# Seven block products of half width in place of four full ones: the second matrix product of an attention and feed-forward kernel

## The chip, the cores and the metric

The kernel runs on one core of one Trainium2 chip. The time is the core's execution time in microseconds (us), the median of several runs. The profile's span runs from the first to the last instruction and is about 2 us shorter than the time. Five engines matter here: TensorE (PE in the profile; its weight loads are PEld), VectorE (DVE), ScalarE (ACT), GpSimd (POOL) and SyncE, whose queue (SPq) issues most transfers.

## The reference, cut to what matters

```python
# batch 8, heads 8, sequence 576, head size 64; window 32
attn = softmax(mask(q @ k.T / 8)) @ v               # per head, only |i - j| <= 32
x    = attn.transpose(0, 2, 1, 3).reshape(4608, 512)
h    = x @ w_in                                      # 512 -> 2048
out  = gelu_tanh(h) @ w_out                          # 2048 -> 512, float32 out
```

## The kernel before

It works through nine tiles of 512 tokens. In tile t the first product (`ffn_in`: 16 x 4 matmuls of 512 columns) and gelu fill `gT`, 2048 features by 512 tokens in f16. The second product (`ffn_out`) makes 64 matmuls of 512 columns from it. Spread among those stands the attention of the next batch: scores (s), masks (m), weighing with the values (v: `ps_o` and `ps_d`), inversion on ScalarE, and spreading of the result into `xT` on VectorE (x). Queries and keys of the batch after that are cast on VectorE, transposed by transfers that SyncE issues, and wanted by the first score in the next second product.

```python
PLAN = {3: ([-1], [0]), 14: ([], [1]), 24: ([0], [2]), 35: ([1], [3]), 46: ([2], [4]), 58: ([3], [])}
# position in the 64 matmuls: (groups to weigh, invert and spread), (groups to score and mask)

def ffn_out(t, t4, fc):
    ...                                              # the last quarter of the last tile in two halves
        nc.tensor.matmul(py[:, cols], gTs[t][:, f, t4 * 128:t4 * 128 + 128],
                         w_out16[:, f, cols], start=(f == 0), stop=(f == NF - 1))
    if f == NF - 1:
        yo = yp.tile([128, 512], FP32, name="yo", tag="yo")
        (nc.scalar.copy if last and half == 0 else nc.vector.tensor_copy)(
            yo[:, cols], py[:, cols])
        ...                                          # one store for each contiguous run of output rows
            eng = nc.scalar if last and m else nc.sync if t else nc.gpsimd
            eng.dma_start(out_v[b, j, q0 + p:q0 + p + e, cols], yo[m:m + e, cols])
```

The softmax here doesn't subtract the row's maximum and nothing guards it: scores larger than these inputs give would overflow.

## Time and profile before

| | |
|---|---|
| time, median of 3 | 323.94 us (323.27 to 325.27) |
| profiled run | 325.46 us, span 323.7 us |
| TensorE busy | 311.7 us, 96% |
| VectorE busy | 136.0 us, 42% |
| one tile of 1 to 6 | 33.6 us: first product 13.8, second product with attention 19.8 |
| from TensorE's end to the end of the span | 3.6 us |

TensorE is busy nearly throughout, so the other engines matter only where TensorE waits for them, and at the end. The profiled run was 1.5 us slower than the median. Where those 1.5 us lie can't be told, as the other runs left no trace. (In the traces of all runs at full clock the start and tile 0 together vary between 60.35 and 63.30 us; tiles 2 to 6 of one kernel mostly repeat within 0.1 us.)

### The profile page before, as it was taken

What the parts mean: (1) busy time and instruction counts of PE and PEld (TensorE: products, weight loads), DVE (VectorE), ACT (ScalarE), POOL (GpSimd) and SP (SyncE); (2) the same over time, 40 slices, a digit from 0 to 9 for tenths busy, and PEclk for the clock granted to TensorE, in tenths of its full rate; (3) what the DMA queues carried; (4) which work ended last, traced back from release to release, by engine and by line L of the source; (5) the groups of instructions that cost most, each with busy time, mean ns of one, the idle gap of its engine ahead of it and who ended that gap; (6) DMA issues with size and microseconds to landing.
All of it is one profiled execution on the core that took longest, in us unless ns stands there. A gap on an engine that the chain in (4) does not pass through costs nothing.

```text
span 323.7 us, 5827 instructions
## 1 busy us (share of the span) xinstructions
PE 311.7 (96%) x2265; PEld 153.4 (47%) x2265; DVE 136.0 (42%) x290; ACT 201.8 (62%) x316; POOL 59.5 (18%) x82
## 2 busy tenths in 40 slices
PE   7688999999999999999999999999999999999995
PEld 2463545444554445444544454445444544444444
DVE  5655587641556064705570467034713530110011
ACT  1757577578667766777577766777668577705600
POOL 3646356292031101300040104010000000000000
PEclk9959999999999999999999999999999999999999
DMA  7999998999989596949495979799270220031022
GB/s 208 259 362 362 381 277 230 251 161 157 248 155 160 95 245 159 169 88 251 115 155 116 221 161 135 134 203 183 75 122 17 67 58 9 0 91 41 0 60 70
DMA packets 120490, 50.57 MB, mean 156 GB/s; under 512 B 100784, under 2 KB 112048, under 8 KB 120464
## 3 DMA queue, kind: packets, MB, share of 16 engines
q1 hardware_dynamic: 88752, 45.07, 58.2%
q0 software_dynamic: 31520, 4.98, 21.0%
q8 instruction: 17, 0.28, 0.4%
q10 hardware_dynamic: 192, 0.16, 0.2%
q14 instruction: 9, 0.07, 0.1%
HBM read 37.62 MB, written 9.44 MB: 145 GB/s over the span
## 4 chain that ended last, share of the span: by engine, by line
PE 93%; SPq 2%; DMA 2%; DVE 1%; ACT 0%; issue 0%; POOL 0%; POOLq 0%
PE mm L461 39%; PE mm L439 24%; PE ph L439 14%; PE ps_o L381 5%; PE ps_s L348 5%; PE ps_d L381 4%; DMA vr<-in_v_dram 2%; SPq L126 1%; PE py L461 1%; ACT gT L443 0%; SPq L135 0%; PE pt L277 0%; DVE w_out L186 0%; PE pt L279 0%; DVE KT L285 0%
## 5 line engine op out<-in xcount | busy, mean ns | idle before, releaser
L461 PE MATMUL mm<-w_out,gT 128*128 128x512 f16 (+1 forms) x576 | 132.0, 377 | 0.8 <-DVE w_out L186 0.8
L439 PE MATMUL mm<-xT,w_in 128*128 128x512 f16 x360 | 89.0, 382 | 0.0
L439 PEld LDWEIGHTS <-w_in 128*128 128x128 f16 x576 | 56.2, 98 | 68.6 <-DVE w_in L186 1.5
L461 PEld LDWEIGHTS <-gT 128*128 128x128 f16 x592 | 54.2, 98 | 61.8 <-issue 0.6
L443 ACT ACTIVATE gT<-mm 128x512 f16<-128x512 f32 x90 | 53.7, 597 | 35.5 <-PE mm L439 35.5
L439 PE MATMUL ph<-xT,w_in 128*128 128x512 f16 x216 | 57.3, 381 | 1.2 <-ACT gT L443 1.2
L354 ACT ACTIVATE pe<-ps_s 128x704 f16<-128x704 f32 x64 | 43.3, 727 | 9.9 <-PE ps_s L348 9.2
L395 ACT ACTIVATE lt<-ps_d 128x480 f32<-128x480 f32 (+3 forms) x40 | 22.2, 555 | 43.2 <-PE ps_d L381 43.1
L443 ACT ACTIVATE gT<-ph 128x512 f16<-128x512 f32 x54 | 32.2, 597 | 13.3 <-PE ph L439 13.3
L405 DVE TENSOR_TENSOR xT<-ps_o,lt 128x480 f16<-128x480 f32 (+5 forms) x38 | 20.3, 552 | 46.9 <-ACT lt L396 46.8
L411 DVE TENSOR_TENSOR xT<-ps_o,lt 128x384 f16<-128x384 f32 (+1 forms) x8 | 4.3, 541 | 80.7 <-ACT lt L396 80.7
L363 DVE TENSOR_TENSOR pe<-pe,mask 128x704 f16<-128x704 f16 x64 | 34.4, 543 | 6.3 <-ACT pe L354 4.0
L465 DVE COPY yo<-mm 128x512 f32<-128x512 f32 x35 | 23.9, 685 | 31.1 <-PE mm L461 28.4
L166 POOL DMA_DIRECT2D V<-in_v_dram x24 | 23.8, 1005 | 63.6 <-PE ps_o L381 47.4
L381 PEld LDWEIGHTS <-V 128*64 128x64 f16 x336 | 18.9, 114 | 18.1 <-issue 11.9
L381 PE MATMUL ps_o<-pe,V 128*64 128x160 f16 (+2 forms) x244 | 22.8, 249 | 1.6 <-POOL V L258 1.5
L396 ACT ACTIVATE lt<-lt 128x480 f32<-128x480 f32 (+3 forms) x40 | 23.5, 588 | 1.3
L381 PE MATMUL ps_d<-pe,ones 128*64 128x192 f16 (+2 forms) x264 | 23.8, 246 | 0.0
L348 PE MATMUL ps_s<-QT,KT 64*128 64x192 f16 (+5 forms) x336 | 19.1, 230 | 2.2 <-DVE KT L285 2.2
L381 PEld LDWEIGHTS <-ones 128*64 128x64 f16 x336 | 19.5, 115 | 0.0
L348 PEld LDWEIGHTS <-KT 64*128 64x128 f16 x336 | 10.9, 95 | 10.6 <-issue 4.2
L168 POOL DMA_DIRECT2D V<-in_v_dram x6 | 5.3, 878 | 56.3 <-PE ps_d L381 39.2
(56 smaller groups left out, 154.3 us busy)
## 6 DMA issues: line engine op xcount, KB each, us to landing
kr<-in_k_dram SPq DMA_DIRECT2D x32, 256.0 KB
qr<-in_q_dram SPq DMA_DIRECT2D x6, 1024.0 KB
V<-in_v_dram POOLq DMA_DIRECT2D x30, 128.0 KB, 5.6
wst<-in_moe_w_in_dram SPq DMA_DIRECT2D x3, 1024.0 KB
wst<-in_moe_w_out_dram SPq DMA_DIRECT2D x3, 1024.0 KB
qr<-in_q_dram SPq DMA_DIRECT2D x8, 256.0 KB
vr<-in_v_dram SPq DMA_DIRECT2D x16, 128.0 KB
out_dram<-yo SPq DMA_DIRECT2D x30, 48.0 KB
```

What stands on the lines that cost most here:

```text
L166: nc.gpsimd.dma_start(V[:, c, :, :], v[b, :, 128 * c:128 * c + 128, :].rearrange("h p d -> p h d"))
L348: nc.tensor.matmul(ps[:, h, off:off + 4 * n].rearrange("k (j p) -> k j p", j=4), KTs[b % 2][r0:r0 + 64, pr, k0:k0 + 128], QTs[b][r0:r0 + 6 ...
L354: nc.scalar.activation(pe, ps[:, :, 0:w], AF.Exp, scale=SCALE)
L363: nc.vector.tensor_tensor(pe, pe, m.rearrange("p (o w) -> p o w", o=1).broadcast_to(list(pe.shape)), op=ALU.mult)
L381: nc.tensor.matmul(bk[r0:r0 + 64, at:at + 4 * n].rearrange("d (j p) -> d j p", j=4)[:, :, p0 - q0:p1 - q0], V[:, c, 2 * pr + h, :] if w == ...
L395: nc.scalar.activation(lt[:, 0:n], d[:, 0:n], AF.Ln)
L396: nc.scalar.activation(lt[:, 0:n], lt[:, 0:n], AF.Exp, scale=-1.0)
L405: nc.vector.tensor_tensor(xT[:, g, pos:pos + e], o[:, done:done + e], lt[:, done:done + e], op=ALU.mult)
L439: nc.tensor.matmul(ph, w_in16[:, dc, fc * 128:fc * 128 + 128], xT[:, dc, t * 512 % RING:t * 512 % RING + 512], start=(dc == 0), stop=(dc = ...
L443: nc.scalar.activation(gTs[t][:, fc, :], ph, AF.Gelu_apprx_tanh)
L461: nc.tensor.matmul(py[:, cols], gTs[t][:, f, t4 * 128:t4 * 128 + 128], w_out16[:, f, cols], start=(f == 0), stop=(f == NF - 1))
L465: (nc.scalar.copy if last and half == 0 else nc.vector.tensor_copy)(yo[:, cols], py[:, cols])
```

## The change

The second product of tiles 1 to 8 is cut into 2 x 2 blocks (tokens, features, output columns each in two halves). Seven block products (`WINO`) replace eight, each of 16 matmuls with 256 columns. The price is sums: S1 to S4 of gelu outputs in every tile, T1 to T4 of weights once, and sums at the eviction, all on VectorE. The plan of the attention gets new positions, weighing and spreading are placed apart, and the gelu table is requested explicitly after the last inversion of a tile.

```diff
-PLAN = {3: ([-1], [0]), 14: ([], [1]), 24: ([0], [2]), 35: ([1], [3]), 46: ([2], [4]), 58: ([3], [])}
+WINO = [("A11", "B11", True), ("S2", "T2", True), ("A12", "B21", False), ("S3", "T3", False),
+        ("S1", "T1", True), ("A22", "T4", False), ("S4", "B22", False)]
+PLAN = {6: "s0 v-1", 24: "s1", 26: "m0", 31: "x-1", 40: "m1", 42: "v0 s2", 48: "x0", 56: "m2",
+        61: "v1 s3", 64: "x1", 80: "m3", 81: "v2 s4", 88: "x2", 97: "v3", 104: "m4", 112: "x3"}
...
+    def combine_w():                                 # called once, at the end of tile 0
+        for dst, x, y in ((T1, B12, B11), (T2, B22, T1)):
+            nc.vector.tensor_tensor(dst, x, y, op=ALU.subtract)
+        ...    todo={17: (T3, B22, B12), 33: (T4, B21, T2)}   # amid tile 1's second product
+    def sums(t, i):                                  # after every fourth gelu
+        for dst, x, y, op in ((S1, A21, A22, ALU.add), (S2, S1, A11, ALU.subtract),
+                              (S3, A11, A21, ALU.subtract), (S4, A12, S2, ALU.subtract)):
+            nc.vector.tensor_tensor(dst, x, y, op=op)
...
+        nc.tensor.matmul(py[:, blk, :], lhsT, wino[w][:, f, :], start=(new and i % 16 == 0),
+                         stop=(i % 16 == 15), skip_group_check=True)
...
+        if n == 0:
+            nc.vector.tensor_copy(M1, py)
+        elif n == 1:
+            nc.vector.tensor_tensor(U2, py, M1, op=ALU.add)
+        elif n == 2:
+            nc.vector.tensor_copy(C11, py)
+        ...                                          # U3, C22, C21 likewise
+        elif n == 5:
+            nc.vector.tensor_tensor(C21, py, M1, op=ALU.add)
+            for x in range(2):
+                store(t, 2 + x, yo[:, 2 + x, :])
+                if end:
+                    store(t, x, yo[:, x, :], left)
```

More of the change, by code (lines that the diff above doesn't have):

```diff
@@ L49 @@
            [(t4, fc) for t4 in (2, 3) for fc in range(16)])
-END = (3, 0, 2, 1)
 RING = 1536
@@ L80, with load_table @@
     exp_set = tabs.index("natural_log_exp_and_others")
-    def load_exp_table():
+    gelu_set = tabs.index("gelu_apprx_tanh_and_others")
+    def load_table(which):
         nc.scalar.add_instruction(mybir.InstLoadActFuncSet(
-            name=nc.get_next_instruction_name(), act_func_set_id=exp_set, ins=[], outs=[]))
+            name=nc.get_next_instruction_name(), act_func_set_id=which, ins=[], outs=[]))
     const = ctx.enter_context(tc.tile_pool(name="const", bufs=1))
@@ L98 @@
     ctx.enter_context(tc.manual_schedule(engines=None))
-    load_exp_table()
+    load_table(exp_set)
     idn = const.tile([128, 128], FP16, name="idn")
@@ L413, in spread, with ffn_in @@
                 lt[:, 0:n].rearrange("d (r q) -> d r q", r=NPAIR), op=ALU.mult)
-    def values(b, g):
-        o, d = weigh(b, g)
-        spread(b, g, o, invert(b, g, d))
     gTs = {}
     phs = {}
-    def ffn_in(t, fc, d0=0, d1=4):
-        if fc == 0 and d0 == 0:
+    def ffn_in(t, n, d0=0, d1=4):
+        fc = n // 2 + 8 * (n % 2) if t else n
+        if n == 0 and d0 == 0:
             gTs[t] = gp.tile([128, NF, 512], FP16, name="gT", tag="gT")
@@ L432, in ffn_in @@
                 if t:
-                    i = (0, 2, 1)[fc % 3] if fc < NF - 1 else 2
+                    i = (first(t), 2, 1 - first(t))[n % 3] if n < NF - 1 else 2
                 else:
@@ L443, in ffn_in, with first @@
             nc.scalar.activation(gTs[t][:, fc, :], ph, AF.Gelu_apprx_tanh)
+            if t and n % 4 == 3:
+                sums(t, n // 4)
+    def first(t):
+        return (t + 1) % 2
+    wino = {}
+    def combine_w():
+        t12 = stage.tile([128, 2, 8, 256], FP16, name="t12", tag="stage")
+        t34 = stage.tile([128, 2, 8, 256], FP16, name="t34", tag="stage")
+        B11, B12, B21, B22 = (w_out16[:, r:r + 8, c:c + 256] for r in (0, 8) for c in (0, 256))
+        T1, T2, T3, T4 = t12[:, 0], t12[:, 1], t34[:, 0], t34[:, 1]
+        for dst, x, y in ((T1, B12, B11), (T2, B22, T1)):
+            nc.vector.tensor_tensor(dst, x, y, op=ALU.subtract)
+        s12 = stage.tile([128, 2, 8, 256], FP16, name="s12", tag="stage")
+        s34 = stage.tile([128, 2, 8, 256], FP16, name="s34", tag="stage")
+        yo = stage.tile([128, 4, 512], FP32, name="y4", tag="stage")
+        wino.update(B11=B11, B21=B21, B22=B22, T1=T1, T2=T2, T3=T3, T4=T4, S1=s12[:, 0],
+                    S2=s12[:, 1], S3=s34[:, 0], S4=s34[:, 1], yo=yo,
+                    todo={17: (T3, B22, B12), 33: (T4, B21, T2)})
@@ new lines, in sums @@
+    def sums(t, i):
+        g, r = gTs[t], slice(2 * i, 2 * i + 2)
+        A11, A21, A12, A22 = (g[:, r0 + 2 * i:r0 + 2 * i + 2, c:c + 256]
+                              for r0 in (0, 8) for c in (0, 256))
+        S1, S2, S3, S4 = (wino[f"S{n}"][:, r, :] for n in (1, 2, 3, 4))
+        for dst, x, y, op in ((S1, A21, A22, ALU.add), (S2, S1, A11, ALU.subtract),
+                              (S3, A11, A21, ALU.subtract), (S4, A12, S2, ALU.subtract)):
+            nc.vector.tensor_tensor(dst, x, y, op=op)
@@ L445 @@
     out_v = out.rearrange("(b p j) f -> b j p f", b=B, j=4)
     pys = {}
-    def ffn_out(t, t4, fc):
-        last = t == NT - 1 and t4 == END[-1]
-        if last:
-            half, fc = divmod(2 * fc, NF)
-            halves = [slice(256 * half, 256 * half + 256)] * 2
-        else:
-            half, halves = 0, [slice(0, 512)]
-        for f, cols in enumerate(halves, fc):
-            if f == 0:
-                pys[t4] = bank((END.index(t4) if t == NT - 1 else t4) % 2) if half == 0 else \
-                    psO.tile([128, 512], FP32, name="py2", tag="O")
-            py = pys[t4]
-            nc.tensor.matmul(py[:, cols], gTs[t][:, f, t4 * 128:t4 * 128 + 128],
-                             w_out16[:, f, cols], start=(f == 0), stop=(f == NF - 1))
-        if f == NF - 1:
-            yo = yp.tile([128, 512], FP32, name="yo", tag="yo")
-            (nc.scalar.copy if last and half == 0 else nc.vector.tensor_copy)(
-                yo[:, cols], py[:, cols])
-            m = 0
-            while m < 128:
-                b, c = divmod(t * 512 + t4 * 128 + m, S)
-                q0, n = (0, cut(b)) if c < 4 * cut(b) else (cut(b), 144 - cut(b))
-                j, p = divmod(c - 4 * q0, n)
-                e = min(n - p, 128 - m)
-                eng = nc.scalar if last and m else nc.sync if t else nc.gpsimd
-                eng.dma_start(out_v[b, j, q0 + p:q0 + p + e, cols], yo[m:m + e, cols])
-                m += e
@@ new lines, in store, with ffn_out_0 @@
+    def store(t, t4, yo, cols=slice(0, 512), eng=None):
+        m = 0
+        while m < 128:
+            b, c = divmod(t * 512 + t4 * 128 + m, S)
+            q0, n = (0, cut(b)) if c < 4 * cut(b) else (cut(b), 144 - cut(b))
+            j, p = divmod(c - 4 * q0, n)
+            e = min(n - p, 128 - m)
+            (eng or nc.sync).dma_start(out_v[b, j, q0 + p:q0 + p + e, cols], yo[m:m + e, cols])
+            m += e
+    def ffn_out_0(t4, fc):
+        if fc == 0:
+            pys[t4] = bank(t4 % 2)
+        nc.tensor.matmul(pys[t4], gTs[0][:, fc, t4 * 128:t4 * 128 + 128], w_out16[:, fc, :],
+                         start=(fc == 0), stop=(fc == NF - 1))
+        if fc == NF - 1:
+            yo = yp.tile([128, 512], FP32, name="yo", tag="yo")
+            nc.vector.tensor_copy(yo, pys[t4])
+            store(0, t4, yo, eng=nc.gpsimd)
@@ new lines, in ffn_out @@
+    def ffn_out(t, i):
+        n, blk, f = i // 16, i // 8 % 2, i % 8
+        if t == 1 and i in wino["todo"]:
+            dst, x, y = wino["todo"][i]
+            nc.vector.tensor_tensor(dst, x, y, op=ALU.subtract)
+        a, w, new = WINO[n]
+        if i % 16 == 0 and new:
+            pys[n % 2] = bank((first(t) + n) % 2)
+        py = pys[n % 2].rearrange("p (b c) -> p b c", b=2)
+        if a[0] == "A":
+            r0, c0 = 8 * (int(a[2]) - 1) + f, 256 * (int(a[1]) - 1) + 128 * blk
+            lhsT = gTs[t][:, r0, c0:c0 + 128]
+        else:
+            lhsT = wino[a][:, f, 128 * blk:128 * blk + 128]
+        nc.tensor.matmul(py[:, blk, :], lhsT, wino[w][:, f, :], start=(new and i % 16 == 0),
+                         stop=(i % 16 == 15), skip_group_check=True)
+        if i % 16 < 15:
+            return
+        yo, left, right = wino["yo"], slice(0, 256), slice(256, 512)
+        C11, C12, C21, C22 = (yo[:, r:r + 2, c] for r in (0, 2) for c in (left, right))
+        end = t == NT - 1
+        M1, U2, U3 = C21, C12, C22
+        if n == 0:
[4 more added lines that the diff above has]
+            nc.vector.tensor_copy(C11, py)
+        elif n == 3:
+            nc.vector.tensor_tensor(U3, py, M1, op=ALU.add)
+        elif n == 4:
+            nc.vector.tensor_tensor(C22, py, U3, op=ALU.add)
+        elif n == 5:
[4 more added lines that the diff above has]
+                    store(t, x, yo[:, x, :], left)
@@ L478, with ffn_last @@
+    def ffn_last(t):
+        py = pys[0].rearrange("p (b c) -> p b c", b=2)
+        yo, right = wino["yo"], slice(256, 512)
+        for x in range(2):
+            nc.vector.tensor_tensor(yo[:, x, right], py[:, x, :], yo[:, x, right], op=ALU.add)
+            store(t, x, yo[:, x, :], right if t == NT - 1 else slice(0, 512))
     cast_open(0)
@@ L573 @@
         ffn_in(0, fc)
-    load_exp_table()
+    load_table(exp_set)
     score(1, 0)
@@ L588 @@
                 ffn_in(t, fc)
-        plan = PLAN if att else {3: ([-1], [])} if t == B - 1 else {}
+        plan = PLAN_0 if not t else PLAN if att else {6: "v-1", 31: "x-1"} if t == B - 1 else {}
         def group(g):
@@ L594 @@
         if plan and t:
-            load_exp_table()
+            load_table(exp_set)
         if t and b + 1 < B:
             load_qk(b + 1)
-        if t == 0:
-            ods = {}
-        for i in range(64):
-            for act in PLAN_0.get(i, "").split() if t == 0 else ():
+        ods = {}
+        for i in range(113 if t else 65):
+            for act in plan.get(i, "").split():
                 kind, g = act[0], int(act[1:])
@@ L623 @@
                     ods[g] = (o, invert(bb, gg, d))
+                    if t and g < 0 and b + 1 < B:
+                        load_v(b + 1)
+                    if t and g == (3 if att else -1):
+                        load_table(gelu_set)
                 else:
                     spread(*group(g), *ods[g])
-            if t and i in plan:
-                for g in plan[i][0]:
-                    values(*group(g))
-                    if g < 0 and b + 1 < B:
-                        load_v(b + 1)
-                for g in plan[i][1]:
-                    score(*group(g))
-                    mask(*group(g))
-            if t:
-                ffn_out(t, END[i // NF] if t == NT - 1 else i // NF, i % NF)
-            else:
-                ffn_out(t, *ORDER_0[i])
+            if t == 0 and i < 64:
+                ffn_out_0(*ORDER_0[i])
+            elif t and i < 112:
+                ffn_out(t, i)
         if t == 0:
+            load_table(gelu_set)
             load_v(2)
+            combine_w()
+        else:
+            ffn_last(t)
         begun = 2 if att else 0
```

## The prediction

> **What bounds the kernel now.** I read the busy shares and slices first, then the chain that ended last in order of time, then the groups by shape, and last VectorE's and SyncE's timelines over one tile (109.8 to 143.4 us).
>
> ```profile
> PE 311.7 (96%) x2265; PEld 153.4 (47%) x2265; DVE 136.0 (42%) x290; ACT 201.8 (62%) x316; POOL 59.5 (18%) x82
> ...
> PE   7688999999999999999999999999999999999995
> ...
> PE 93%; SPq 2%; DMA 2%; DVE 1%; ACT 0%; issue 0%; POOL 0%; POOLq 0%
> ```
>
> TensorE is busy in every slice from the fourth on, and the chain is TensorE for 93% of the span. So time is won by giving TensorE less to do, if nothing new makes it wait. Its price per matmul comes from the chain in order of time (start, length, what):
>
> ```profile
> 97.87 1.73 PE mm L439 x8
> 99.60 0.86 PE ph L439 x4
> 100.46 1.73 PE mm L439 x8
> ...
> 318.36 1.76 PE py L461 x16
> 320.12 0.02 issue
> 320.14 0.42 DVE yo L465
> ```
>
> Twelve 512-column matmuls take 100.46 - 97.87 = 2.59 us, 0.216 us each. The sixteen 256-column ones at the end, each with new weights, take 1.76 / 16 = 0.110 us each: half the columns cost half, and the weight load (98 ns) still hides. A tile from 1 to 6 takes 143.4 - 109.8 = 33.6 us: 64 + 64 matmuls of the two products are 27.65, the attention of the next batch the other 5.95. The period holds no visible TensorE gap.
>
> The kernel ends with a small eviction (0.42) and the last store: TensorE stops issuing at about 319.94 and the span ends at 323.7, a tail of 3.76 us.
>
> VectorE durations that the change multiplies, from the groups by shape:
>
> ```profile
> L363 DVE TENSOR_TENSOR pe<-pe,mask 128x704 f16<-128x704 f16 x32 | 17.9, 558 | 4.5 <-ACT pe L354 4.0
> L465 DVE COPY yo<-mm 128x512 f32<-128x512 f32 x35 | 23.9, 685 | 31.1 <-PE mm L461 28.4 <-DMA out_dram<-yo 2.8
> L405 DVE TENSOR_TENSOR xT<-mm,lt 128x512 f16<-128x512 f32 x2 | 1.4, 692 | 1.4 <-ACT lt L396 1.4
> L465 DVE COPY yo<-py 128x256 f32<-128x256 f32 x1 | 0.4, 425 | 2.8 <-PE py L461 2.8
> ```
>
> The f16 masks take 558 ns at 704 and 524 at 640 elements: 0.53 ns per element and about 185 fixed, so a 512-element f16 sum is estimated at 0.46 us and a 2048-element one at 1.27. A 512-element f32 instruction out of PSUM is 0.69, whether copy or sum.
>
> **What the Trainium skill says.** "TensorE: Matmul & The Clock Gate" (Wait — 56ns, not 53.3ns?) gives N / 2.4 GHz plus about 2.5 ns: 215.8 ns for 512 columns and 109.2 for 256. The trace agrees (216 and 110). The same page's Back-to-back issue gap has about 131 ns for a stream of 512-column pairs; this trace contradicts it, and I use 216. "VectorE: DVE Perf Modes" (The perf-mode tier table) allows tensor_tensor two elements a cycle on 16-bit SBUF operands and one with PSUM; 0.53 ns per element and 692 ns agree. "ScalarE: Activation LUTs" (What ACT_TABLE_LOAD costs) has 1283 ns for a load, as here (1283); the further 1380 ns of drain isn't visible: Ln starts 0.02 us after a load.
>
> **TensorE, part by part.** In each of tiles 1 to 8 the 64 matmuls of 512 columns (13.82 us) become 7 x 16 = 112 of 256 columns: 112 x 0.110 = 12.32. That is 1.50 us per tile, 12.0 over eight tiles, all on the path. Tile 0 and the first product keep their matmuls. The floor without new waits or tail is 323.94 - 12.0 = 311.9.
>
> **The gelu table.** In the trace the load before the tile's first gelu runs at 129.62 to 130.90, directly after the last inversion, and the gelu then waits 0.40 us for its matmul. It's already early. Asking for it by hand gains nothing: 0.
>
> **VectorE.** Added per tile: 16 sums of gT, 16 x 0.46 = 7.4 us; four copies (2.74) become two copies, four 512 sums and two 256 sums, 6 x 0.69 + 2 x 0.42 = 5.0. Together 9.6 us per tile, 77 in all, plus four weight sums of 1.27. VectorE goes from 136 to about 218 us, near 70%: not the bound on average. The first-product stage holds 6.2 us today and gets three of the four sum groups, 5.5: 11.7 of 13.8. The second-product stage goes from 8.9 to about 13.0 of 18.3. So the question is order: VectorE works in program order, and PSUM has only two banks for block products and one for attention outputs.
>
> I walked one tile (2 to 6) by hand with these durations, 0 being the start of its second product. The last gelu ends at 0.84, the last sum group at 2.7; its S2 is ready by 1.8, before product 1 starts at 2.7. Product 0 is copied out by 3.6, product 2 wants its bank at 4.85: free. Products 3, 4, 5 and 6 want banks that were read at 6.0, 8.6, 11.7 and 13.5, at 7.7, 10.8, 12.7 and 15.3: all free. What binds is the attention's output bank: the second weighing (position 61) could start at 9.16, but the spreading that frees its bank is queued behind the eviction of product 2 and ends at 9.28; the last weighing likewise waits for 15.5. With signalling, some 0.18 + 0.13 = 0.31 us per tile, 1.55 over tiles 2 to 6. The last spreading ends at about 18.4 and the next tile asks for it at 19.3. Tile 7 has nearly no attention and tile 8 none: 0.
>
> Tile 1 also computes T3 and T4 on VectorE amid its evictions. Each shifts what follows by 1.27: the first weighing waits about 0.6, the second about 1.3, and with the usual last wait tile 1 loses 2.1. T1 and T2 at the end of tile 0 delay the casts by 2.5, which have slack: the transposed keys would be there some 2 us ahead.
>
> **The stores.** SyncE issues them, in order. In the tail of before, the first five stores run back to back:
>
> ```profile
> 310.46 0.75 SPq L474 DMA_DIRECT2D out_dram<-yo  x2
> 310.83 1.20 SPq L474 DMA_DIRECT2D out_dram<-yo  x3
> ```
>
> From 310.46 to 312.4 that is about 0.395 each, and the last one, issued at 320.6, ends the span 3.1 us later. Before, tile 8 spreads 13 stores over 10 us and puts the last two on two queues. After, nothing leaves until product 5 is evicted. With T the end of TensorE's issuing: product 5 ends at T - 1.76, is seen 0.2 later and is added in 0.69, so the first store starts at T - 0.84. There are 11, then 4 more that need the last two sums (ready at T + 1.04): SyncE is the slower. The fifteenth starts at T - 0.84 + 14 x 0.395 = T + 4.7 and lands at T + 7.8, against T + 3.76 before: 4.0 us given back, on the path. Each store also waits for one of eight completion counters, so the ninth needs the first to have landed (T + 2.3 by then, about the time it is due); under load this could add 1 to 2 us. In earlier tiles the same burst sits ahead of the transposes on SyncE, pushing them from 3.3 to about 4.2 us after the tile's start; the first score needs the first key pair at 14.5, and it lands near 12: hidden.
>
> **Sum.** 323.94 - 12.0 (matmuls) + 0 (table) + 1.55 (tiles 2 to 6) + 2.1 (tile 1) + 4.0 (tail) = 319.6 us.
>
> **Rivals.**
> First, VectorE's order becomes the bound: every wait in my walk that just fits is missed by some tenths. For it: VectorE would be over 70% full in the second-product stage, in order, between two engines. Against: the evictions have 1 to 2 us of slack. With 1 us lost in each of tiles 2 to 6 instead of 0.31 it makes 323.
> Second, the matmul saving arrives whole, because the plan's positions were chosen for these durations, and the weight sums fit: 311.9 plus the tail of 4.0, 316, faster by 2.4%. For it: banks come free early in my walk. Against: the output bank's margins there are negative, by tenths.
> Third, the transposes slip past the first score, since the DMA engines are over 90% busy in alternate slices and SyncE fills about 27 us of each period (transposes 11, loads 10, stores 4 to 6). A slip of 3 us beyond my estimate would cost 1 us in each of six tiles: 325. The 2 us of slack and a stage that shortens by only 1.5 us speak against it.
> Fourth, a busier weight path (LDWEIGHTS 98 ns of each 110) misses under waits, 2 ns per matmul: 896 x 2 ns = 1.8 us more. The sixteen 0.110 us pairs at the end speak against it.
>
> **Range and chances.** Without any stall 316; with doubled stalls (3.7 more) 323. I take 316.2 to 322.6 for 8 in 10. Faster by over 2% means below 317.5: the stalls would have to be under a third of mine, or the tail be nearly what it was: 0.20. Slower by over 2% means above 330.4, which needs the third rival twice over: 0.02. Within 2%: 0.78.
>
> **What would show it.** Right: 256-column pairs at 0.110 us; a second-product stage of about 18.3 to 18.6 us in tiles 2 to 6 and 12.3 in tile 8; TensorE waits on VectorE's spreading at the second and last weighing, most in tile 1; VectorE near 218 us; fifteen stores ending about 7.8 us after the last matmul. Wrong: sums of gT at 0.69 instead of 0.46 us (then the last sum group is late for product 1); TensorE waiting for evictions rather than for spreadings; a tail under 5 us; scores waiting for keys.

## The result

| | before | after |
|---|---|---|
| time, median | 324.0 us (4 runs, 323.27 to 325.27) | 319.99 us (4 runs, 319.71 to 321.32) |
| ratio | | 0.988 (0.9838 to 0.9922): within 2% |
| profiled span | 323.7 us | 317.7 us |

A ratio here is the mean time of one kernel's fast runs over that of the other's from the same rounds, so it isn't quite the ratio of the medians. The prediction, 319.6 us, was met within 0.4 us. The parts below show that this is partly luck.

First the page of the changed kernel: busy time of the engines, TensorE and its granted clock in 40 slices of the span, and the chain that ended last by engine.

```profile
PE 299.7 (94%) x2633; PEld 189.5 (60%) x2633; DVE 201.8 (64%) x454; ACT 200.7 (63%) x315; POOL 59.1 (19%) x82
...
PE   6688999997999999999999999999999999999990
...
PEclk9959999999799999999999999999999999999996
...
PE 85%; DVE 5%; DMA 4%; SPq 3%; issue 1%; ACT 1%; POOL 0%; DVEq 0%; POOLq 0%
```

TensorE's busy time fell by 12.0 us, VectorE's rose by 65.8. TensorE is no longer busy in the last slice, and in the tenth slice (about 71 to 79 us) it falls to 7, with the granted clock down to 7 in the slice after. The chain now has 5% VectorE and 4% DMA in it, where it had 1% and 2%.

To see where the time went I take TensorE's first matmul of each tile's first product as a mark, in both traces.

| stretch | before | after | difference | predicted |
|---|---|---|---|---|
| start and tile 0 | 62.38 | 62.25 | -0.13 | 0 |
| tile 1 | 33.60 | 35.87 | +2.27 | +0.6 |
| tiles 2 to 6 | 168.03 | 159.08 | -8.95 | -5.95 |
| tile 7 | 28.26 | 26.67 | -1.59 | -1.5 |
| tile 8 | 27.83 | 26.20 | -1.63 | -1.5 |
| from TensorE's end | 3.6 | 7.6 | +4.0 | +4.0 |
| sum | 323.7 | 317.7 | -6.0 | -4.35 |

The two profiled runs differ by 6.0 us and the medians by 4.0: before's profiled run lay 1.5 us above its median, and after's was the fastest of its four.

**Tile 1.** The chain of the changed kernel in order of time shows the new piece (start, length, what):

```profile
62.45 0.69 DVE yo L500
63.15 1.14 DVE t L462
...
65.52 1.88 DVE q L309 x4
67.40 2.09 DVE qt L309 x4
69.49 1.34 DVE k L317 x4
...
72.73 6.42 DMA KT<-k
79.16 0.05 issue
79.21 0.46 PE ps_s L352 x8
80.17 3.65 PE mm L518 x18
...
145.41 2.07 PE mm L518 x18
...
297.84 12.24 PE mm L518 x112
```

Read upwards: the first score (79.21) waited for the transposed keys, their transfer (72.73 to 79.15) for SyncE's issue, the issue for the casts of queries and keys, and those for T1 and T2 (L462), which VectorE had to do first. TensorE's waits put the gap down to the keys: label, us in total, times, longest.

```profile
PE ps_s L352 <- DMA KT<-k: 2.3, 1, 2.3
```

SyncE's timeline of both kernels shows the shift itself (start, length, what it issues). Before:

```profile
64.74 3.60 SPq L308 DMA_TRANSPOSE QT<-q  x1
68.43 1.17 SPq L308 DMA_TRANSPOSE QT<-qt  x1
69.70 5.41 SPq L314 DMA_TRANSPOSE KT<-k  x4
```

After:

```profile
67.47 3.89 SPq L312 DMA_TRANSPOSE QT<-q  x1
71.46 1.18 SPq L312 DMA_TRANSPOSE QT<-qt  x1
72.73 5.30 SPq L318 DMA_TRANSPOSE KT<-k  x4
```

The keys are issued 72.73 - 69.70 = 3.0 us later; the first product ends at the same time in both kernels (within 0.2 us). After the wait TensorE was also slow for a while: its chain has 18 block-product matmuls in 3.65 us from 80.17, where the same 18 take 2.07 in tile 3 (145.41). That is 1.6 us more. The first score starts 16.95 us after the tile's first matmul, 2.4 us later than in a quiet tile (14.56), and the second weighing slips by another 0.1. So tile 1 lost 2.4 + 1.6 + 0.1 against a quiet tile of 31.8 us: 35.9, and 35.87 was measured.

**The other tiles.** Product matmuls and VectorE's new instructions, from the groups by shape of the changed kernel:

```profile
L478 DVE TENSOR_TENSOR s<-gT 128x512 f16<-128x512 f16 x64 | 26.9, 420 | 41.1 <-ACT gT L445 41.1
L528 DVE COPY y<-mm 128x512 f32<-128x512 f32 x8 | 5.5, 690 | 6.8 <-PE mm L518 6.8
L548 DVE TENSOR_TENSOR y<-mm,y 128x256 f32<-128x256 f32 x16 | 6.0, 417 | 2.1 <-PE mm L518 2.1
```

The f16 sums take 0.42 us (0.46 was estimated), and in the timeline those of a group that don't need the sum just before them start 0.34 us after it. The evictions take 0.69 and 0.42, as in the estimate. The last tile's 112 matmuls stand in the chain as one piece of 12.24 us from 297.84 (the last line of the chain above): 0.1093 each. TensorE's waits in tiles 2 to 6 hold nothing of this stage.

**The tail.** The changed kernel's timeline at its end:

```profile
309.08 6.16 SPq L490 DMA_DIRECT2D out_dram<-y  x15
310.11 0.76 DVE L548 TENSOR_TENSOR y<-mm,y 128x256 f32<-128x256 f32 x2 [1.05 <-PE mm L518]
```

SyncE issues fifteen stores in 6.16 us, 0.41 each, beginning 0.99 us before TensorE's end at 310.07. The last starts near 314.8, and the span ends at 317.7.

### The profile page after: what moved, and what is told of

It is laid out like the page before. It is cut to its first block, busy times and chain, and to the rows that moved or that the text cites. A ratio compares the mean times of both kernels' runs of the same rounds, so it can differ in the third digit from the quotient of the medians.

```text
span 317.7 us, 6698 instructions
## 1 busy us (share of the span) xinstructions
PE 299.7 (94%) x2633; PEld 189.5 (60%) x2633; DVE 201.8 (64%) x454; ACT 200.7 (63%) x315; POOL 59.1 (19%) x82
## 4 chain that ended last, share of the span: by engine, by line
PE 85%; DVE 5%; DMA 4%; SPq 3%; issue 1%; ACT 1%; POOL 0%; DVEq 0%; POOLq 0%
PE mm L518 32%; PE mm L441 22%; PE ph L441 13%; PE ps_o L385 5%; PE ps_s L352 4%; PE mm L496 4%; PE ps_d L385 4%; DMA KT<-k 2%; SPq L130 2%; DMA vr<-in_v_dram 2%; DVE qt L309 1%; DVE q L309 1%; ACT gT L445 0%; DVE s L478 0%; DVE pe L367 0%
## 5 line engine op out<-in xcount | busy, mean ns | idle before, releaser
L518 PEld LDWEIGHTS <-s 128*128 128x128 f16 x512 | 48.9, 98 | 8.0
L478 DVE TENSOR_TENSOR s<-gT 128x512 f16<-128x512 f16 x64 | 26.9, 420 | 41.1 <-ACT gT L445 41.1
L518 PE MATMUL mm<-t,s 128*128 128x256 f16 x384 | 47.2, 275 | 0.0
L518 PEld LDWEIGHTS <-gT 128*128 128x128 f16 x384 | 36.4, 99 | 7.8
L170 POOL DMA_DIRECT2D V<-in_v_dram x24 | 23.9, 1010 | 55.4 <-PE ps_o L385 41.7
L367 DVE TENSOR_TENSOR pe<-pe,mask 128x704 f16<-128x704 f16 x64 | 32.6, 546 | 2.3 <-ACT pe L358 2.3
L518 PE MATMUL mm<-w_out,gT 128*128 128x256 f16 x256 | 33.9, 279 | 0.0
L87 ACT ACT_TABLE_LOAD x17 | 21.8, 1283 | 1.1 <-PEq L728 0.8
L352 PE MATMUL ps_s<-QT,KT 64*128 64x192 f16 (+5 forms) x336 | 18.2, 230 | 4.4 <-DMA KT<-k 2.3
```

The costliest lines, as they stand in the source:

```text
L87: nc.scalar.add_instruction(mybir.InstLoadActFuncSet(name=nc.get_next_instruction_name(), act_func_set_id=which, ins=[], outs=[]))
L170: nc.gpsimd.dma_start(V[:, c, :, :], v[b, :, 128 * c:128 * c + 128, :].rearrange("h p d -> p h d"))
L352: nc.tensor.matmul(ps[:, h, off:off + 4 * n].rearrange("k (j p) -> k j p", j=4), KTs[b % 2][r0:r0 + 64, pr, k0:k0 + 128], QTs[b][r0:r0 + 6 ...
L367: nc.vector.tensor_tensor(pe, pe, m.rearrange("p (o w) -> p o w", o=1).broadcast_to(list(pe.shape)), op=ALU.mult)
L478: nc.vector.tensor_tensor(dst, x, y, op=op)
L518: nc.tensor.matmul(py[:, blk, :], lhsT, wino[w][:, f, :], start=(new and i % 16 == 0), stop=(i % 16 == 15), skip_group_check=True)
```

## The experiments

Twelve kernels ran, five rounds each (a median is over all runs of a kernel, 5 or 6 unless said otherwise). All gave correct results. Kernels of a batch share the runs of the kernel before: 324.70 us in the first batch, 324.97 in the second, 325.38 and 324.72 in the third and fourth. Theory: the gain in the product stages came whole, tile 1 lost it through T1 and T2 delaying the keys, and the stores lost 4 us. Rivals: VectorE's order in the second product is the bound (T3, T4, the second weighing); the throttle of TensorE's clock costs the time by itself; or tiles 2 to 6 gained by new positions of the attention rather than by fewer matmul columns.

### after_again: the changed kernel once more

No edit.

> The changed kernel itself, beside the others and with a second profile. Expected 320 us (319.7 to 321.3). If the loss in tile 1 is a fixed part of the kernel, the profile shows again a wait of about 2.3 us for the transposed keys before the first score of tile 1 (the period of tile 1 about 35.9 us against 31.8 of tiles 2 to 6). If it was an accident of one run, tile 1 takes about 32 us here. The half clock after that wait may come or not: the mean clocks of the first four runs differed (0.970 to 0.984).

Measured: 320.80 us (318.09 to 321.43), ratio 0.986 (0.983 to 0.989). In its profile tile 1 took 37.87 us: the keys were waited for 3.45 us, and the half-speed stretch followed again. Tiles 2 to 6 took 31.8 each, as in the first profile. So the wait in tile 1 is no accident of one run, but its size varies by over a microsecond; of the two profiled runs the one with the longer wait took longer (321.09 against 319.71 us).

### e1_t12_late: T1 and T2 after the casts

```diff
             if att and b > 1:
                 cast_and_turn(b)
+            if t == 1:
+                combine_w()
...
-            combine_w()                              # at the end of tile 0
```

> T1 and T2 are computed after the casts of tile 1 instead of before them; nothing else moves. Theory A (the result's trace): the two sums hold the casts up by 2.5 us, so the keys' transposes land after the first score wants them; here the wait of 2.3 us goes and with it the half clock that followed (1.7 us), so the run is 2.5 to 4 us faster than the changed kernel, about 316.5, and the period of tile 1 falls from 35.9 to 32 to 33.4. Theory B (as the prediction had it): tile 1 loses through T3 and T4 amid the evictions; then nothing changes here, 320, or the 2 us of waits at the first and second weighing only come to light in place of the wait for keys.

Measured: 316.12 us (315.12 to 317.49), ratio 0.973 (0.971 to 0.976), faster. Tile 1 took 32.27 us: neither the wait nor the half speed. The two weight sums are still computed by VectorE in tile 1, only behind the casts instead of ahead of them. What cost the time was therefore their place ahead of the casts, not their length. Elsewhere a wait of 0.4 us for keys came up once, in tile 5.

The cost of T3 and T4 can be read in the same run, now undisturbed, from TensorE's timeline (in brackets: idle before, and what ended it):

```profile
85.35 0.26 PE L385 MATMUL ps_o<-pe,V 128*64 128x160 f16 x2 [0.36 <-DVE xT L409]
```

The second weighing waits 0.36 us for the spreading. In all tile 1 lost 0.47 us here against a quiet tile (32.27 against 31.80), and that is the whole cost of T3 and T4, where I had put 0.6 and 1.3.

### e6_keep_busy: TensorE kept at work while it waits

```diff
+            if t == 1 and i == 6:
+                keep(10)          # ten matmuls of 512 columns into the attention's idle bank
```

> Ten matmuls of 512 columns whose result nobody reads (2.2 us) stand in front of the first score of tile 1, where TensorE otherwise waits 2.3 us for the keys. If the slow matmuls after the wait come from the wait itself (TensorE idle, clock halved), TensorE keeps full clock here and the run gains up to 1.7 us: about 318.3, with a mean clock near 0.984. If the slow stretch has another cause, or the filler only delays the score, the time is 320 or more.

Measured: 319.16 us (316.88 to 322.39), ratio 0.980 (0.977 to 0.983), unclear. Only four of its six runs count as fast, and the profiled one (322.39) doesn't, so its trace is used here for lengths of waits and not for the time. TensorE's timeline, two places:

```profile
76.03 2.32 PE L483 MATMUL spin<-w_in 128*128 128x512 f16 x10
79.55 0.46 PE L352 MATMUL ps_s<-QT,KT 64*128 64x160 f16 x8 [1.20 <-DMA KT<-k]
...
80.41 1.27 PE L523 MATMUL mm<-w_out,gT 128*128 128x256 f16 x10
...
209.62 0.46 PE L352 MATMUL ps_s<-QT,KT 64*128 64x160 f16 x8 [2.26 <-DMA KT<-k]
...
210.48 1.91 PE L523 MATMUL mm<-w_out,gT 128*128 128x256 f16 x10
```

In tile 1 the filler shortened the idle time to 1.20 us, and the ten product matmuls after it took 1.27 us. In tile 5 no filler was there, the same wait lasted 2.26 us, and ten matmuls took 1.91. So the slow stretch follows the idle time, not the block products or the tile. It's a cost of the wait, not a cause by itself. But a wait doesn't always bring it. In the profile of e3 (below), which has the same matmuls but for the filler, TensorE waited longer and then ran at full speed:

```profile
78.64 0.46 PE L352 MATMUL ps_s<-QT,KT 64*128 64x160 f16 x8 [3.31 <-DMA KT<-k]
...
79.49 1.27 PE L518 MATMUL mm<-w_out,gT 128*128 128x256 f16 x10
```

That the filler saved the slow stretch of tile 1 is therefore not shown by this one profile. "TensorE: Matmul & The Clock Gate" (What's actually happening) of the Trainium skill gives half clock after at least one idle window of about 3.4 us. The half speed agrees (the recorded clock was 0.5 for 3.4 us from 80.0 on in the profile of the changed kernel); the length alone doesn't decide: 2.3 us of idleness were enough there, and 3.31 us in e3 weren't. What decides isn't shown by these runs.

### e4_tail: stores as soon as their quarter is final

```diff
         elif n == 2:
             nc.vector.tensor_copy(C11, py)
+            if end:
+                for x in range(2):
+                    store(t, x, yo[:, x, :], left)
...      # likewise C22 after product 4; the last six of tile 8 partly on ScalarE's queue
-                if end:
-                    store(t, x, yo[:, x, :], left)
+                    store(t, 2 + x, yo[:, 2 + x, :], left, eng=(nc.scalar, nc.sync)[x])
```

> Only the stores of tile 8 are moved: each quarter of the output leaves as soon as it is final, and the last ones go half over ScalarE's queue. Theory: the tail is 15 stores of 0.4 us each on one queue behind the last but one eviction; here 7 are left after it on two queues and 4 after the last sums, so the last is issued about 1.5 us after TensorE's end instead of 4.8, and the span's tail falls from 7.6 to about 4.5 us: 317 us. Rival: the tail is the time that the transfers themselves take (1 MB, mostly after TensorE's end); then it falls by less than 1 us.

Measured: 317.23 us (316.04 to 320.87), ratio 0.976 (0.974 to 0.978), faster. The profiled run is its slow one (320.87; tile 1 with a key wait of 3.1 us), so only its tail is read: 5.9 us instead of 7.6. That is 1.7 us, of the 3.0 to 3.8 by which the median of its fast runs (316.97) lies below the two medians of the changed kernel (319.99 and 320.80). The rest may be the varying wait in tile 1; this run doesn't settle it. SyncE still had most of the late stores to issue.

### e5_both: e1, and the last stores over two queues

```diff
+            if t == 1:
+                combine_w()                          # as in e1
...
             nc.vector.tensor_tensor(C22, py, U3, op=ALU.add)
+            if end:
+                for x in range(2):
+                    store(t, 2 + x, yo[:, 2 + x, :], right, eng=(nc.sync, nc.scalar)[x])
...      # the rest as in e4
```

> T1 and T2 after the casts, and the stores of tile 8 spread: each quarter leaves when it is final, with SyncE and ScalarE sharing so that behind the last but one eviction each queue has at most 7 left (in the run before only ScalarE's queue was short, and SyncE still issued 14 in 6.15 us, so the tail fell from 7.6 to 5.9 only). If tail and key wait are separate losses, they add: 4.1 us from the one, about 3 from the other, 313 us, with a span's tail of about 4.7 us. If both came from the same busy DMA, the gain is less than 5 us in all.

Measured: **312.60 us** (311.85 to 313.12), ratio **0.962** (0.960 to 0.964). It beats both kernels. The timeline of its end (the queues of ScalarE and SyncE, then the last sums):

```profile
305.01 2.89 ACTq L490 DMA_DIRECT2D out_dram<-y  x7
305.67 2.85 SPq L490 DMA_DIRECT2D out_dram<-y  x7
306.70 0.76 DVE L555 TENSOR_TENSOR y<-mm,y 128x256 f32<-128x256 f32 x2 [1.05 <-PE mm L518]
```

Two queues issue seven stores each in under 3 us, where one took 6.16 us for fifteen. From TensorE's end (306.66) to that of the span (311.0) there are 4.3 us, against 7.6: 3.3 us less, and the median is 3.5 us below e1's. So 3.3 of the tail's 4.0 us were won back by order and queue alone. Tile 1 of this run still waited 1.57 us for the keys, without a slow stretch after it (33.90 us). So moving T1 and T2 doesn't remove the wait in every run: the first keys took 8.4 us from issue to landing here, against 6.4 in the profile of the changed kernel.

### e8_copy_twice: one eviction doubled (on top of e1)

```diff
         elif n == 2:
             nc.vector.tensor_copy(C11, py)
+            nc.vector.tensor_copy(C11, py)
```

> As with T1 and T2 after the casts, but the eviction of product 2 is done twice (the same 0.69 us copy once more) in every tile from 1 to 8. The prediction's walk has the second weighing wait for the spreading queued behind this very eviction: then each of tiles 1 to 6 loses 0.5 to 0.7 us, tiles 7 and 8 none, 3 to 4 us in all (about 320). If VectorE has slack there, the time stays at 316.

Measured: 320.40 us (319.30 to 321.53), ratio 0.987 (0.984 to 0.989). Each of tiles 2 to 6 took 32.5 us instead of 31.8, that is 0.7 more for one 0.69 us copy. TensorE's waits name it:

```profile
PE ps_o L385 <- DVE xT L409: 4.4, 6, 1.1
```

VectorE's path from that eviction to the second weighing has thus no slack at all, as the prediction's walk had it, but no negative slack either: without the doubled copy there is no such wait in tiles 2 to 6. (In tile 1 this run, too, waited for keys, 0.99 us, with T1 and T2 moved.)

### e3_no_gelu_ask: without the requests for the gelu table

```diff
-                    if t and g == (3 if att else -1):
-                        load_table(gelu_set)
...
-            load_table(gelu_set)                     # end of tile 0
```

> The changed kernel without its requests for the gelu table (the load then stands where it stood before, ahead of the first gelu). Theory: it's worth nothing, since the load was early before too; same time as the changed kernel within 0.3%, 320 to 321. Rival: it hides 0.4 to 1.3 us per tile; then 3 us or more slower.

Measured: 318.91 us (317.88 to 322.34), ratio 0.985 (0.981 to 0.989), not to be told from the changed kernel (0.986). The key wait of tile 1 was 3.31 us in its profile. ScalarE's timeline without the request:

```profile
127.21 0.60 ACT L400 ACTIVATE lt<-lt 128x480 f32<-128x480 f32 x1
127.83 1.28 ACT L445 ACT_TABLE_LOAD   x1
```

The load still starts 0.02 us after the last inversion ends. It was put in ahead of the gelu, which waits for its matmul, and itself waits for nothing.

### e7_before_replan: the kernel before with new positions

```diff
-PLAN = {3: ([-1], [0]), 14: ([], [1]), 24: ([0], [2]), ...
+PLAN = {4: ([], [0]), 5: ([-1], []), 16: ([], [1]), 24: ([0], [2]), ...
```

> The kernel before with its own second product, but with the order that the change gives to the attention's start: scores of group 0 first, then the weighing of the last tail (one matmul later than before), and the scores of group 1 at 16 instead of 14. In the trace of before these two places cost TensorE about 0.15 us each per tile. Theory: that part of what tiles 2 to 6 gained beyond the block products (0.3 us of the 1.8) is had without them: 1.5 to 2 us faster than before, 0.5%. Rival: the extra gain came from the block products themselves; then no change.

Measured: 324.80 us (323.61 to 327.86, 14 runs), ratio 1.000 (0.998 to 1.003). Tiles 2 to 6 took 33.5 instead of 33.6 us. I had hoped to find the 0.3 us per tile by which the changed kernel gained more than I had predicted; 0.12 of it is here (33.61 to 33.49 in tiles 3 to 6). These positions alone don't give the gain. Other positions weren't tried. Tile 1 of this profile waited 1.15 us for the keys, in a kernel that computes none of the new sums: the keys of tile 1 have little slack even without T1 and T2.

### e9_keys_first and e12_keys_second: another order of casts and transposes (on e5)

```diff
-        for src, dst in ((qr, q16), (qt, qt16)):     # casts and transpose of queries, then their tail
-            ...
-        for pr in range(NPAIR):                      # then each pair of keys
-            ...
+        keys(0)                                      # e9: the first pair of keys, then queries,
+        queries(qr, q16)                             #     other keys, tail of the queries
+        for pr in range(1, NPAIR): keys(pr)
+        queries(qt, qt16)
```

In e12 the order is `queries(qr, q16)`, all `keys(pr)`, `queries(qt, qt16)`.

> As the run with both repairs (312.6 us), and the first key pair is cast and transposed ahead of the queries, the tail of the queries last, so what the first score of a tile needs is issued 1.2 us earlier. In the profile of the run with both repairs tile 1 still waited 1.6 us for keys (period 33.9 us against 31.8). Theory: that rest of the key wait goes, with any half clock behind it: 1 to 2 us faster, 311. Rival: the landing of the transposes is set by the busy DMA engines and not by the order of issue; then 312.6 again.

> As the run with both repairs (312.6 us), but the keys are cast and transposed right behind the queries, and the tail of the queries (needed only for group 4) last. Putting keys ahead of the queries did not help (316.7): the first score needs both, and then it's the queries that come late. Here nothing that the first score needs is later than in the run with both repairs, and the keys are issued 1.2 us earlier. If the order of issue counts, the rest of the key wait in tile 1 (1.6 us in that run's profile) shrinks to 0.4 or less: 311 to 312. If the landing is set by the busy DMA engines, 312 to 314 as before.

Measured: e9 316.51 us as the median of its five fast runs (313.19 to 317.14; 316.66 with the slow one), ratio 0.972 (0.968 to 0.976), slower than e5. Its profiled run fell into a throttled state (385.79 us at a mean granted clock of 0.753), so its trace explains nothing, and why it is slower isn't shown by it. e12: 312.81 us (311.43 to 314.81), ratio 0.965 (0.962 to 0.968), as e5. In e12's profile the wait for keys is gone and tile 1 takes 32.89 us, but two waits of 0.6 and 0.4 us for the spreading are left there. So the 1.57 us of e5's profile are no reserve that this order wins: over five and six runs the two kernels are the same.

### e10_t34_pool and e11_all: T3 and T4 on GpSimd (on e5, and on e9's order)

```diff
-                    todo={17: (T3, B22, B12), 33: (T4, B21, T2)})
+                    todo={})
+        for dst, x, y in ((T3, B22, B12), (T4, B21, T2)):
+            nc.gpsimd.tensor_tensor(dst, x, y, op=ALU.subtract)
```

> As the run with both repairs, but T3 and T4 are computed on GpSimd ahead of tile 1's second product, not on VectorE amid its evictions. The prediction gave these two sums 2.1 us of waits in tile 1; the run with T1 and T2 moved shows only about 0.5 us (period of tile 1 32.3 against 31.8). If that is right, at most 0.5 us is gained: 312 to 312.6. If the waits were 2.1 us and hidden, 310.5. If GpSimd is too slow or gets in VectorE's way, slower than 312.6.

> All of it together: T1 and T2 after the casts, T3 and T4 on GpSimd, keys first, stores of tile 8 spread. If the three rests of tile 1 are separate, its period comes to 31.8 to 32 us and the time to about 310.5 to 311.5; if not, no better than the better of the two runs beside it.

Measured: e10 320.82 us (fast runs 319.24 to 321.05, and one of 378.53), ratio 0.986 (0.983 to 0.989): 8.2 us slower than e5. Tile 1 took 41.69 us. The timeline of GpSimd there:

```profile
67.43 4.11 POOL L469 TENSOR_TENSOR t<-w_out 128x2048 f16<-128x2048 f16 x1
77.06 4.17 POOL L469 TENSOR_TENSOR t<-w_out,t 128x2048 f16<-128x2048 f16 x1 [5.51 <-PE ps_s L352]
```

And of VectorE:

```profile
65.83 7.00 DVE L309 CAST qt<-qt 16x512 f16<-16x512 f32 x4 [2.39 <-DMA qt<-in_q_dram]
...
77.34 4.16 DVE L479 TENSOR_TENSOR s<-s,gT 128x512 f16<-128x512 f16 x1
```

While a GpSimd sum of 4.1 us runs, VectorE stands: a sum of 0.42 us that began 0.28 us into it takes 4.16, and the casts that overlap the other one take 7.00. TensorE then waits 5.9 us in all for the sums of gelu outputs. "SBUF — State Buffer" (SBUF: two separate sides) of the Trainium skill calls the port pair that the two engines share "an exclusive lock, not a bandwidth split", which a VectorE operation with two SBUF inputs or in a two-port mode takes as well. This trace agrees. e11: 321.55 us (320.74 to 323.03), ratio 0.990 (0.987 to 0.993), with the same lock, tile 1 at 42.3 us, and its first score waiting 1.9 us, now for the queries. A late arrival of the queries may be what slowed e9 too; e9's own trace can't say.

## Why the prediction was right, and where it was so by luck

**The sum** was right (319.6 predicted, 319.99 measured), and both large terms in it were right: the matmuls and the tail. Between them two terms of the sum failed, in opposite directions.

**The matmuls, 1.50 us per tile: right.** They measured 12.24 us per 112, so 13.82 - 12.24 = 1.58. Tiles 7 and 8, which hold little or no attention, gained 1.59 and 1.63. The rival that a busier weight path misses is refuted: 0.1093 us each.

**The waits of 0.31 us per tile in tiles 2 to 6: wrong, there are none.** The step "the spreading that frees its bank is queued behind the eviction of product 2 and ends at 9.28" was right in kind and a fraction too pessimistic. e8 shows the margin is about zero: 0.69 us put into that path came out as 0.72. The walk's sums were 0.46 us each, and they take 0.42 and partly overlap; that this is what made the walk too pessimistic is argued. VectorE had 12.1 us of work in the second-product stage of 18.0 (13.0 of 18.3 was predicted), and 202 us in all (218). "The period holds no visible TensorE gap" also missed two small waits of about 0.1 us each per tile before. A tile gained 1.79 us, 1.58 of it by the matmuls; of the other 0.21, e7's new positions gave 0.12 without any block product, and the rest is argued from the two timelines. Together tiles 2 to 6 gained 8.95 us instead of 5.95.

**T1 and T2 "delay the casts by 2.5, which have slack: the transposed keys would be there some 2 us ahead": wrong, and this was the worst step.** The casts were delayed by 65.52 - 63.19 = 2.3 us, so the delay was right. The slack wasn't. The first key pair took 6.42 us from issue to landing, as the chain shows, in a slice of the page in which the DMA engines were over 90% busy. Issued at 69.70, as in before, and with the same 6.42 us, it would have landed at 76.1, about 0.7 us before its score's turn (62.25 + 14.56 = 76.8): an estimate from these numbers, in place of the 2 us. TensorE waited 2.3 us, and a stretch near half speed cost 1.6 more. The third rival named this wait, but for every tile and as a slip of SyncE (at a cost of 6 us, which makes 325.6, not 325). In the two profiles of the changed kernel it came in tile 1 only (0.06 us in tile 5 of the second aside), from VectorE's order. e1 takes that cause away and gains 4.7 us on the median (320.80 to 316.12).

**The burst of stores ahead of the transposes, "from 3.3 to about 4.2 us": too small.** In tiles 2 to 6 of the changed kernel SyncE issues the queries' transposes 3.7 to 6.4 us after the tile's start. Mostly that stays hidden. In tile 5 of e6 it didn't; SyncE's timeline there:

```profile
191.09 8.18 SPq L495 DMA_DIRECT2D out_dram<-y  x11
199.38 4.33 SPq L312 DMA_TRANSPOSE QT<-q  x1
```

The queries had been cast by 195.5, but SyncE was issuing stores until 199.3. The first keys left 12.7 us after the tile's start, and TensorE waited the 2.26 us shown under e6; in tile 5 of e1 it waited 0.36 in the same way. So the slip that the third rival feared exists, in single tiles of some runs. No run moved these stores.

**T3 and T4, 2.1 us: mis-sized, 0.5 us.** They do delay the spreading ahead of the second weighing as described, but only 0.47 us of it reaches TensorE (e1's trace, with tile 1 undisturbed), and 0.1 in the changed kernel, where the second weighing comes after the wait for the keys. In the changed kernel tile 1 lost 4.1 us against a quiet tile, by another way than predicted.

**The table, 0: right** (e3). **The tail, 4.0 us: right**, by the steps given. The prediction's T, the end of issuing, lies about 0.16 us before TensorE's end (319.94 against 320.1 in before). From it, the first store started at T - 0.83 (T - 0.84 predicted), each took 0.41 us instead of 0.395, and the end came at T + 7.8, as predicted. The completion counters added nothing visible. e5 shows that 3.3 of the 4.0 us are no property of the change.

So the second rival (316, no stalls) was closest to the truth of tiles 2 to 8, and the wait in tile 1 brought the sum back near my figure. Two things stay open. The changed kernel scatters between 318.1 and 321.4 us, which the varying wait in tile 1 (2.3 and 3.45 us in two profiles), the slow stretch that follows or doesn't, and the varying start and tile 0 may explain, but runs without a profile can't show it. And where the last 0.1 us per tile in tiles 2 to 6 went isn't settled.

## What to carry to other kernels

Less work for the engine that bounds the kernel pays one to one as long as the helpers' in-order queues keep their deadlines, so look not at their busy share but at what stands behind each added instruction: 2.3 us put ahead of casts that start a chain of transfers cost 4 us in the profiled run, and moved behind them about 0.5 in e1's. Take the time from issue to landing of a transfer from the loaded stretch where it runs, not from a quiet one. Where a change gathers results so that they become final late, send each part when it is final and over more than one queue: that alone gave back 3.3 us.

## What the Trainium skill lacked or had wrong

- "TensorE: Matmul & The Clock Gate" (Back-to-back issue gap) has about 131 ns per matmul for a stream of 512 columns; here such a stream takes 216 ns each, and 109.3 ns at 256 columns with new weights every time.
- "TensorE: Matmul & The Clock Gate" (What's actually happening) has the half clock after an idle window of about 3.4 us. Here an idle time of 2.3 us was followed by it (18 matmuls in 3.65 us instead of 2.07), also 2.26 us in e6; 3.31 us in e3, 1.57 in e5 and 1.2 in e6 were not. So the length of one idle time doesn't tell by itself. The section also calls the window free-running; whether the place of the idle time in it decides, no run here shows.
- "VectorE: DVE Perf Modes" (The three transpose paths) has 1309 ns for a DMA transpose of 128 x 128. Four such blocks in one transfer took 6.42 us from issue to landing with the DMA engines over 90% busy. The page says nothing of the time under load, which decided this case.
- "VectorE: DVE Perf Modes" (The DRAIN you can't avoid) has the next operation wait until the pipe is empty unless it's not held; f16 sums of 0.42 us that don't use the sum just before them started 0.34 us after it here, the one that does 0.46. The section has no figure for how much earlier.
- "ScalarE: Activation LUTs" (What ACT_TABLE_LOAD costs) has about 1380 ns of drain after the 1283 ns of a load; here the next operation started 0.01 us after a load.
- "GPSIMD Engine Reference" has 4497 ns for a sum of 2048 elements in fp32; in f16 a difference of as many took 4.11 us here (GpSimd's spans are rough), so 16 bits hardly help. The page has no 16-bit figure.
